# Top-k attention with a low-rank mixer: masking of the probabilities moved from VectorE to GpSimd, row sums to ScalarE

## The chip, the cores and the metric

The kernel runs on one core of one Trainium2 chip. The time is that of one execution on the device, in microseconds (us). The engines have short names: PE is TensorE (matmuls and transposes; PEld is its weight load), DVE is VectorE, ACT is ScalarE, POOL is GpSimd, SP is SyncE, which issues loads.

## The reference

For each of 8 batches and 8 heads (576 rows, 64 columns), attention keeps the 32 largest scores of a row. What follows is an MLP-mixer block on the joined heads.

```python
scores = scale * np.matmul(q, k.transpose(0, 1, 3, 2))
kth = np.partition(scores, -top_k, axis=-1)[..., -top_k:-top_k + 1]
mask = scores >= kth
scores = np.where(mask, scores, -1000000000.0)
scores = scores - np.max(scores, axis=-1, keepdims=True)
attn = np.exp(scores)
attn = attn / (np.sum(attn, axis=-1, keepdims=True) + 1e-09)
out = np.matmul(attn, v)
# x: heads joined, (8, 576, 512)
h = x.transpose(0, 2, 1) @ U @ V          # rank 32
u = x + h.transpose(0, 2, 1)
result = u + np.maximum(u @ w_ch1, 0.0) @ w_ch2
```

## The kernel before

Heads are taken in pairs, so there are 32 pairs, four to a batch. The 576 rows of a pair are five tiles: four of 128 rows and a tail of 64. A *step* is one tile of one pair, 160 in all. A full step has two chunks of 128 x 576 scores, one for each head. A tail step has one chunk, which holds the 64 rows of both heads one above the other. Every five steps are called a *group* here.

A step has a front and a back. The front, `scores` and `select`, makes the scores with four matmuls (L209), copies them to a tile `Ssb` in SBUF on ACT (L219, in the tail L222), and finds the 32nd largest score of each row on DVE: four rounds of the eight largest values (`MAX8`, L233) with three removals of these between them (`MATCH_REPLACE8`, L242, into tiles `rr`). After the first round ACT makes the exponentials `E` (L237, L238). After the last round the eighth value `ms[c][:, 7:8]` is the threshold, and one DVE instruction for each chunk (L245) compares the scores with it, multiplies `E` with the result, and accumulates the row sums, with a small DVE instruction that reads the accumulator out. In the tail step DVE adds 1e-9 to the sum and inverts it (L265, L266), and POOL scales `E` (L267); in full steps this is done later, on the attention's output (L311 to L316).

The back transposes `E` on PE (L288), copies the result on ACT (L289), and multiplies with the values (L295), with a copy of the output on ACT (L304).

The main loop puts the front of step n ahead of the back of step n - 1. Between these, `fill` lays pieces of the MLP of the batch before: w1 matmuls (L382) with a Relu on ACT (L392), and w2 matmuls (L399), whose output DVE adds (L409) and POOL sends out (L411). After the fourth pair of a batch the mixer is laid in (L336, L349, with DVE's additions at L350). In the first 19 steps two pieces of the weights in 64 bits are also rounded in every step, by five DVE and three POOL instructions each (L108 to L124).

PE's instructions stand in the order in which the program names them, so PE meets, in this order: the scores of step n, a piece of MLP, the transposes of step n - 1 with MLP between them, the scores of step n + 1. A PE instruction that waits holds all that is behind it. The other engines have queues that run in order too, but that order is made by a planner, which takes what it reckons to be ready first, by its own costs. Tiles come from pools; `bufs` says how many of one kind are alive at once, and a new tile waits for all readers of the one whose place it takes.

The lines that the change touches are in `scores` and `select`:

Of the kernel before, what the change touches and what calls it, by code (L numbers as in the profile page):

```python
# [8 lines left out]
F32 = mybir.dt.float32  # L9
U32 = mybir.dt.uint32  # L10
AF = mybir.ActivationFunctionType
ALU = mybir.AluOpType
# [8 lines left out]
def kernel(  # L21
# [23 lines left out]
    nc = tc.nc  # L45
    B, H, S, D = q.shape
    P = 128
# [16 lines left out]
    attn = ctx.enter_context(tc.tile_pool(name="attn", bufs=2))  # L64
# [15 lines left out]
    def rows(t):  # L80
        return P if t < NT else TAIL

    def cols(t):
        return slice(t * P, t * P + rows(t))

    def half(h):
        return slice(h * D, (h + 1) * D)
# [112 lines left out]
    def scores(g, t):  # L200


        qkT = qkTs[g]
        n = rows(t)
        S2 = attn.tile([P, 2, S], F32, tag="Ssb", name="Ssb", bufs=2)
        scs = [ps_s.tile([P, 2, 512], F32, tag="sc", name="sc") for _ in range(2)]
        for i, sc in enumerate(scs):
            for h in range(2):
                nc.tensor.matmul(  # L209
                    sc[slice(0, n) if t < NT else half(h), h, 0:HALF],  # L210
                    lhsT=qkT[half(h), 0, cols(t)],
                    rhs=qkT[half(h), 1, i * HALF : (i + 1) * HALF],
                    start=True,
                    stop=True,
                )
        for i, sc in enumerate(scs):
            cs = slice(i * HALF, (i + 1) * HALF)
            if t < NT:
                nc.scalar.copy(S2[:, :, cs], sc[:, :, 0:HALF])  # L219
            else:  # L220
                for h in range(2):
                    nc.scalar.copy(S2[half(h), 0, cs], sc[half(h), h, 0:HALF])  # L222
        return [S2[:, 0], S2[:, 1]] if t < NT else [S2[:, 0]]

    def select(chunks, sums):


        Es = [attn.tile([P, S], F32, tag="E", name="E", bufs=6) for _ in chunks]
        curs, ms = list(chunks), [None] * len(chunks)
        for i in range(TOPK // 8):  # L230
            for c in range(len(chunks)):
                m = small.tile([P, 8], F32, tag="m8", name="m8")
                nc.vector.max(m, curs[c])  # L233
                ms[c] = m
                if i == 0:
                    nmax = small.tile([P, 1], F32, tag="nmax", name="nmax", bufs=4)
                    nc.scalar.mul(nmax, m[:, 0:1], -SCALE)  # L237
                    nc.scalar.activation(Es[c], chunks[c], AF.Exp, bias=nmax, scale=SCALE)  # L238
            if i < TOPK // 8 - 1:
                for c in range(len(chunks)):  # L240
                    nxt = attn.tile([P, S], F32, tag="rr", name="rr", bufs=4)
                    nc.vector.match_replace(nxt, ms[c], curs[c], NEG)  # L242
                    curs[c] = nxt
        for c in range(len(chunks)):
            nc.vector.scalar_tensor_tensor(  # L245
                out=Es[c],
                in0=chunks[c],
                scalar=ms[c][:, 7:8],
                in1=Es[c],
                op0=ALU.is_ge,  # L250
                op1=ALU.mult,
                accum_out=sums[c],
            )
        return Es

    def front(g, t):
        if t == 0:
            dens[g] = small.tile([P, NT, 2], F32, tag="den", name="den", bufs=3)
        chunks = scores(g, t)
        if t < NT:  # L260
            probs[g, t] = select(chunks, [dens[g][:, t, h : h + 1] for h in range(2)])
        else:
            den = small.tile([P, 1], F32, tag="dent", name="dent", bufs=2)
            (E,) = select(chunks, [den])
            nc.vector.tensor_scalar_add(den, den, 1e-9)  # L265
            nc.vector.reciprocal(den, den)  # L266
            nc.gpsimd.tensor_scalar(E, E, den, None, ALU.mult)  # L267
            probs[g, t] = [E]
            del qkTs[g]
# [247 lines left out]
```

## Time and profile before

| | before |
|---|---|
| median of 3 runs | 2250.36 us (2250.21 to 2250.86) |
| profiled execution | 2251.6 us |
| its span | 2249.8 us |
| DVE busy | 1822.1 us (81%) |
| PE busy | 1953.6 us (87%) |
| ACT busy | 866.0 us (38%) |
| POOL busy | 235.5 us (10%) |
| mean granted PE clock | 0.908 |

The profile is one execution. In a row for a group of instructions stand the line, the engine, the operation, what is written and read, and the count; then the busy time in us and the mean duration in ns; then the idle time of the engine just before them and what ended it. In a timeline a row starts with the start and the length in us, and instructions of one kind that follow each other are merged. A row of the windows view has the stretch, its length, the busy time of PE, PEld, DVE, ACT and POOL with the count of instructions, the granted PE clock, the DMA share and GB/s. In the rows with 40 digits each digit is a slice of the span; 9 is a busy share of 90% or more, and for the clock it is tenths of full speed.

### The profile page before, as it was taken

The numbers are of one execution on the slowest core, as the hardware profiler recorded it, in microseconds if no ns is written. First come the engines' busy times: TensorE is split into PE (matmuls) and PEld (weight loads), VectorE is DVE, ScalarE is ACT, GpSimd is POOL, SyncE is SP. The second block draws the span as 40 slices with busy tenths as digits, with TensorE's granted clock in tenths as the row PEclk, the third lists the DMA queues.
The fourth block names the chain that finished last, engine by engine and source line by source line (L and its number), as shares of the span: only waits on it lengthen the run. The fifth ranks groups of instructions, "written<-read, shape, count | busy, mean of one in ns | idle before, by whom it ended". The sixth has DMA issues, their size and how long they took to land.

```text
span 2249.8 us, 27480 instructions
## 1 busy us (share of the span) xinstructions
PE 1953.6 (87%) x10048; PEld 1141.4 (51%) x10048; DVE 1822.1 (81%) x3876; ACT 866.0 (38%) x2001; POOL 235.5 (10%) x186
## 2 busy tenths in 40 slices
PE   5334448999899989999899989999899989999998
PEld 3223234656365645646365645647365645546545
DVE  8999997999599995999599976999699968996000
ACT  3223233445254533444254434444244424443100
POOL 2655530000000000000000000000000000000000
PEclk6556558999899998999899989999899989999999
DMA  3222210100000000010000000000000000000000
GB/s 83 80 76 64 79 35 4 24 27 18 10 21 21 24 21 16 17 28 17 10 22 21 24 16 23 20 26 19 5 22 21 24 16 26 1 10 3 10 12 10
DMA packets 98630, 56.59 MB, mean 25 GB/s; under 512 B 83712, under 2 KB 92064, under 8 KB 98496
## 3 DMA queue, kind: packets, MB, share of 16 engines
q1 hardware_dynamic: 95552, 45.40, 7.6%
q0 software_dynamic: 2944, 9.44, 1.2%
q8 instruction: 79, 1.29, 0.2%
q14 instruction: 55, 0.45, 0.1%
HBM read 45.38 MB, written 9.44 MB: 24 GB/s over the span
## 4 chain that ended last, share of the span: by engine, by line
DVE 46%; PE 36%; issue 13%; ACT 4%; DMA 0%; POOL 0%; SPq 0%; POOLq 0%; DVEq 0%; ACTq 0%
DVE m L233 19%; DVE rr L242 17%; PE mm L399 13%; PE mm L382 8%; PE O L295 5%; DVE E L245 4%; PE sc L209 4%; PE tp L288 3%; PE mm L349 2%; ACT Ssb L219 2%; DVE bits L114 1%; ACT E L238 1%; ACT PT L289 1%; DVE bits L111 1%; DVE X L316 1%
## 5 line engine op out<-in xcount | busy, mean ns | idle before, releaser
L399 PE MATMUL mm<-w,hT 128*128 128x512 f32 (+1 forms) x1280 | 619.0, 616 | 3.5 <-DVE X L350 3.5
L233 DVE MAX8 m<-rr 128x8 f32<-128x576 f32 x864 | 614.1, 747 | 1.9
L382 PE MATMUL mm<-uT,w 128*128 128x256 f32 (+1 forms) x2048 | 545.4, 412 | 1.5 <-ACT hT L392 1.4
L382 PEld LDWEIGHTS mm<-uT,w 128*128 128x128 f32 x2048 | 372.5, 190 | 123.4 <-issue 32.9
L242 DVE MATCH_REPLACE8 rr<-m,rr 128x576 f32<-128x576 f32 x576 | 423.4, 741 | 0.0
L288 PE MATMUL tp<-ident,E 128*128 128x128 f32 (+1 forms) x1440 | 246.9, 299 | 196.2 <-DVE E L245 131.8
L288 PEld LDWEIGHTS tp<-ident,E 128*128 128x128 f32 (+1 forms) x1440 | 175.1, 145 | 343.8 <-DVE E L245 134.8
L399 PEld LDWEIGHTS mm<-w,hT 128*128 128x128 f32 (+1 forms) x1280 | 215.3, 184 | 247.8 <-issue 241.5
L289 ACT COPY PT<-tp 128x512 f32<-128x512 f32 (+1 forms) x448 | 209.5, 495 | 320.0 <-PE tp L288 319.1
L233 DVE MAX8 m<-Ssb 128x8 f32<-128x576 f32 x288 | 205.5, 749 | 137.2 <-ACT Ssb L219 136.0
L295 PE MATMUL O<-PT,va 128*64 128x128 f32 (+3 forms) x3200 | 236.8, 288 | 19.7 <-ACT PT L289 18.9
L295 PEld LDWEIGHTS O<-PT,va 128*64 128x64 f32 (+1 forms) x3200 | 173.0, 146 | 113.4 <-issue 60.1
L245 DVE SCALAR_TENSOR_TENSOR E<-Ssb,m,E 128x576 f32<-128x576 f32 x288 | 223.4, 808 | 3.5
L238 ACT ACTIVATE E<-Ssb,nmax 128x576 f32<-128x576 f32 x288 | 223.0, 774 | 6.4
L392 ACT ACTIVATE hT<-mm 128x320 f32<-128x320 f32 (+1 forms) x256 | 104.3, 407 | 288.7 <-PE mm L382 288.0
L242 DVE MATCH_REPLACE8 rr<-m,Ssb 128x576 f32<-128x576 f32 x288 | 211.8, 742 | 0.0
L209 PE MATMUL sc<-qkT 64*128 64x288 f32 (+1 forms) x1280 | 210.3, 450 | 0.3 <-ACT qkT L188 0.3
L219 ACT COPY Ssb<-sc 128x576 f32<-128x576 f32 x256 | 152.3, 640 | 117.9 <-PE sc L209 115.3
L409 DVE TENSOR_TENSOR ob<-X,mm 128x512 f32<-128x512 f32 (+1 forms) x40 | 27.3, 682 | 188.8 <-PE mm L399 188.8
L209 PEld LDWEIGHTS sc<-qkT 64*128 64x128 f32 (+1 forms) x1280 | 110.0, 187 | 89.7 <-issue 66.2
L237 ACT ACTIVATE nmax<-m 128x1 f32<-128x1 f32 x288 | 56.5, 196 | 232.8 <-DVE m L233 232.3
L267 POOL TENSOR_SCALAR E<-E,dent 128x576 f32<-128x576 f32 x32 | 56.7, 1772 | 802.3 <-DVE dent L266 755.0
(53 smaller groups left out, 976.0 us busy)
## 6 DMA issues: line engine op xcount, KB each, us to landing
raw<-in_moe_w_ch_dram SPq DMA_DIRECT2D x32, 512.0 KB, 3.7
ld_q<-in_q_dram SPq DMA_DIRECT2D x64, 128.0 KB, 2.7
ld_k<-in_k_dram SPq DMA_DIRECT2D x64, 128.0 KB, 2.7
va<-in_v_dram SPq DMA_DIRECT2D x64, 128.0 KB, 2.1
out_dram<-ob POOLq DMA_DIRECT2D x32, 256.0 KB, 2.6
ld_q<-in_q_dram SPq DMA_DIRECT2D x32, 32.0 KB, 2.4
ld_k<-in_k_dram SPq DMA_DIRECT2D x32, 32.0 KB, 2.4
va<-in_v_dram SPq DMA_DIRECT2D x32, 32.0 KB, 2.2
```

The costliest lines, as they stand in the source:

```text
L209: nc.tensor.matmul(sc[slice(0, n) if t < NT else half(h), h, 0:HALF], lhsT=qkT[half(h), 0, cols(t)], rhs=qkT[half(h), 1, i * HALF : (i + 1 ...
L219: nc.scalar.copy(S2[:, :, cs], sc[:, :, 0:HALF])
L233: nc.vector.max(m, curs[c])
L238: nc.scalar.activation(Es[c], chunks[c], AF.Exp, bias=nmax, scale=SCALE)
L242: nc.vector.match_replace(nxt, ms[c], curs[c], NEG)
L245: nc.vector.scalar_tensor_tensor(out=Es[c], in0=chunks[c], scalar=ms[c][:, 7:8], in1=Es[c], op0=ALU.is_ge, op1=ALU.mult, accum_out=sums[c],)
L288: nc.tensor.transpose(tp[0 : rows(j), j - j0, h, :], E[:, cols(j)], ident)
L289: nc.scalar.copy(PT[0:n, j0 : js[-1] + 1, 0:nh, :], tp[0:n, 0 : len(js)])
L295: nc.tensor.matmul(O[half(h), 0:m], lhsT=va[0 : rows(j), h, j, :], rhs=PT[0 : rows(j), j, h, :] if nh == 2 else PT[0 : rows(j), j, 0, half ...
L382: nc.tensor.matmul(ph[:, 0:width], lhsT=w1[:, cc, f * P : (f + 1) * P], rhs=uT[:, cc, 0:width], start=(cc == 0), stop=(cc == NC - 1),)
L392: nc.scalar.activation(hTs[f][:, 0:width], ph[:, 0:width], AF.Relu)
L399: nc.tensor.matmul(po[0:n, :], lhsT=hTs[f][:, offs[t] : offs[t] + n], rhs=w2[:, f, :], start=(f == 0), stop=(f == NF - 1),)
```

## The change

For each chunk the one DVE instruction is replaced by three on other engines: POOL compares the scores with the threshold into a new tile `top`, POOL multiplies `E` by it, and ACT copies `E` onto itself while it accumulates the row sum. `Ssb` gets a third buffer, and `rr` has three instead of four.

```diff
-        S2 = attn.tile([P, 2, S], F32, tag="Ssb", name="Ssb", bufs=2)
+        S2 = attn.tile([P, 2, S], F32, tag="Ssb", name="Ssb", bufs=3)
...
-                    nxt = attn.tile([P, S], F32, tag="rr", name="rr", bufs=4)
+                    nxt = attn.tile([P, S], F32, tag="rr", name="rr", bufs=3)
...
         for c in range(len(chunks)):
-            nc.vector.scalar_tensor_tensor(
-                out=Es[c],
-                in0=chunks[c],
-                scalar=ms[c][:, 7:8],
-                in1=Es[c],
-                op0=ALU.is_ge,
-                op1=ALU.mult,
-                accum_out=sums[c],
-            )
+            top = attn.tile([P, S], F32, tag="top", name="top")
+            nc.gpsimd.tensor_scalar(top, chunks[c], ms[c][:, 7:8], None, ALU.is_ge)
+            nc.gpsimd.tensor_tensor(Es[c], Es[c], top, ALU.mult)
+            nc.scalar.activation(Es[c], Es[c], AF.Copy, accum_out=sums[c])
         return Es
```

## The prediction

> **What bounds the kernel now.** I read the page's engine rows and its slices first.
>
> ```profile
> PE 1953.6 (87%) x10048; PEld 1141.4 (51%) x10048; DVE 1822.1 (81%) x3876; ACT 866.0 (38%) x2001; POOL 235.5 (10%) x186
> PE   5334448999899989999899989999899989999998
> DVE  8999997999599995999599976999699968996000
> PEclk6556558999899998999899989999899989999999
> ```
>
> There are three stretches. Up to 327 us (steps 0 to 19) DVE is full, PE half idle. From there to 2060 us both are nearly full. The last 190 us are MLP on PE alone. In the middle a batch of 20 steps holds three ordinary five-step groups of 54.6, 56.0, 54.6 us (mean 55.1, from the timeline) and one of 83.6 us in which the mixer runs: seven batches, so 21 ordinary groups and 7 of the other kind. The windows view takes one ordinary group, then two clock windows:
>
> ```profile
> 650.40:705.00 54.60, 52.83 (x299) 31.31 (x298) 52.27 (x114) 26.61 (x62) 1.75 (x2) 1.00 0.08 22
> 1088.10:1091.52 3.42, 1.98 (x4) 0.66 (x4) 3.42 (x8) 0.17 (x1) 0.00 (x0) 1.00 0.00 0
> 1091.52:1094.93 3.41, 1.14 (x2) 0.63 (x3) 2.81 (x7) 0.00 (x0) 0.00 (x0) 0.50 0.00 0
> ```
>
> PE is busy 52.83 and DVE 52.27 of 54.60 us: neither has room. The other two rows show what a gap costs: PE was busy 1.98 of 3.42 us, and the next window's granted clock was 0.50.
>
> Next, the order of one step, on PE (scores, transposes, scores two steps on) and on DVE (first maximum, the two maskings, the next step's first maximum), and who waited in 345 to 2054 us:
>
> ```profile
> 650.44 1.24 PE L209 MATMUL sc<-qkT 64*128 64x288 f32 x8
> 663.82 1.15 PE L288 MATMUL tp<-ident,E 128*128 128x128 f32 x8
> 671.41 1.24 PE L209 MATMUL sc<-qkT 64*128 64x288 f32 x8
> ```
> ```profile
> 652.45 1.42 DVE L233 MAX8 m<-Ssb 128x8 f32<-128x576 f32 x2 [2.83 <-ACT Ssb L219]
> 662.11 0.80 DVE L245 SCALAR_TENSOR_TENSOR E<-Ssb,m,E 128x576 f32<-128x576 f32 x1
> 662.84 0.81 DVE L245 SCALAR_TENSOR_TENSOR E<-Ssb,m,E 128x576 f32<-128x576 f32 x1
> 664.18 1.41 DVE L233 MAX8 m<-Ssb 128x8 f32<-128x576 f32 x2
> ```
> ```profile
> PE tp L288 <- DVE E L245: 7.4, 24, 0.7
> ```
>
> Masking ends at 663.65 and the transposes start at 663.82; still PE waited only 7.4 us for E in 1700. E arrives just in time, with no reserve. The ring is: scores to first maximum 2.0; to the end of the last maximum (662.19) 9.7; to the transposes 1.6; to the scores two steps on 7.6. That is 20.9 us for two steps, while DVE needs 22.8 for them (652.45 to 675.29). So DVE sets the pace by 1.9 us, and PE's own work (21.0, 650.44 to 671.41) is as close behind.
>
> **Prices.** From the groups, shapes kept apart:
>
> ```profile
> L245 DVE SCALAR_TENSOR_TENSOR E<-Ssb,m,E 128x576 f32<-128x576 f32 x288 | 223.4, 808 | 3.5
> L238 ACT ACTIVATE E<-Ssb,nmax 128x576 f32<-128x576 f32 x288 | 223.0, 774 | 6.4
> L219 ACT COPY Ssb<-sc 128x576 f32<-128x576 f32 x256 | 152.3, 640 | 117.9 <-PE sc L209 115.3
> L267 POOL TENSOR_SCALAR E<-E,dent 128x576 f32<-128x576 f32 x32 | 56.7, 1772 | 802.3 <-DVE dent L266 755.0 <-PE O L295 23.7 <-PE mm L399 17.4
> L121 POOL TENSOR_SCALAR mask<-mask 128x512 f32<-128x512 f32 x32 | 64.5, 2016 | 109.5 <-DVE mask L119 109.5
> L124 POOL TENSOR_TENSOR w<-bits,mask 128x512 f32<-128x512 f32 x32 | 42.8, 1336 | 2.5
> ```
>
> *Removed:* 288 maskings and accumulator reads, 223.4 + 23.4 = 247 us of DVE, 1.5 us of a full step.
>
> *Compare:* same operation, shape and column operand as L267, whose median is 1.72. Ends: 1.43 (were it as quick as a product) and 2.27 (2016 scaled by 576/512; L121 runs against DVE). I take 1.72. *Product:* L124's undisturbed 1.27 scaled by 576/512 is 1.43. *Row sum on ACT:* between the 0.64 of L219 and the 0.77 of L238; 0.70 and 0.10 for the accumulator (0.08 on DVE). ACT gains 230 us on 866 and stays far from full.
>
> *The chain of a full step,* from the end of the second chunk's last maximum: the first chunk's is 0.66 earlier, start on POOL 0.20 (dent at 1010.37, L267 at 1010.57), compare 1.72, hand-over 0.07, product 1.43, the same 3.22 for the second chunk, to ACT 0.15, row sum 0.80, to PE 0.10. Sum 7.0, where now it is 1.6: PE's transposes read what ACT writes, so they wait for all of it. Tail step (one chunk): 0.20 + 3.22 + 0.95, then add, reciprocal, L267 and hand-overs 2.5: 6.9 against 3.4 now.
>
> *Buffers:* with three rr, the fourth and sixth MATCH_REPLACE8 output reuses a tile read by the instruction just before; 0 to 0.14 each (tail step's spacing 0.80 against 0.66), I take 0.1, so the 9.7 becomes 9.9. The third Ssb lets the next copies go while POOL still reads; without it that read would hold them.
>
> *The ring after:* 2.0 + 9.9 + 7.0 + 7.6 = 26.5 us for two steps, above DVE's (about 20) and PE's 21.0. So PE idles 5.5 us per two steps. The row at 1088.10 says that 1.44 idle in a window halves the clock. At the batch change PE restarted at 605.65 and had 1.00 back at 610.2: 4.6 us at half speed lose 2.3. This lies in the stretch from transposes to scores: 28.8. Tail ring, from step 74: copies done 2.4 after the scores (1000.49 to 1002.85), maxima 5.5 (1002.88 to 1009.05 less an output add of 0.67), 6.9, and 5.7 to the scores (1014.8 to 1020.5): 20.5, with clock 22.8. Ten steps are eight full and two tail legs on two chains: (8 x 28.8 + 2 x 22.8)/2 = 138.0, or 69.0 per group, 13.9 more than 55.1. Times 21: +292.
>
> The Trainium skill ("TensorE: Matmul & The Clock Gate", Part 1) has the half clock come after an idle window of about 3.4 us; the row above fell with 1.98 us busy, so the row decides. By the page alone shorter gaps would keep the clock, which is the first rival's sum.
>
> The Trainium skill ("GPSIMD Engine Reference", Engine selection) calls one-input work on GPSIMD roughly line-rate; L267's 1.72 against MAX8's 0.75 on as many elements denies it. With a compare of about 0.7, the estimate by that page, a full leg is 2.0 shorter and the total some 95 us lower.
>
> *Mixer groups:* their first two steps have E ready 22 to 30 us ahead (580.0 against 605.7), so nothing is added; the last three are ordinary: 0 to 3 x 2.8; I take 4, times 7: +28.
>
> *First stretch:* DVE does the step, then rounds two weights. Here it shares something with POOL:
>
> ```profile
> 152.90 0.68 DVE L111 SCALAR_TENSOR_TENSOR bits<-raw,bits 128x512 uint32<-128x512 uint32 x1
> 153.50 1.48 DVE L119 TENSOR_SCALAR mask<-raw 128x512 uint32<-128x512 uint32 x1
> ```
> ```profile
> 151.37 2.06 POOL L121 TENSOR_SCALAR mask<-mask 128x512 f32<-128x512 f32 x1 [8.88 <-DVE mask L119]
> 153.41 1.29 POOL L118 TENSOR_TENSOR bits<-bits,last 128x512 uint32<-128x512 uint32 x1
> ```
>
> L119 takes 1.48 beside POOL's two-input operation, 0.41 alone; L111 beside the one-input one keeps its 0.68. MAX8 and MATCH_REPLACE8 don't change beside either. Masks now run just when DVE rounds: two products cost 1.1 each, against 1.3 saved (1.5 less 0.2): +0.9 on 16 steps, about +15. Ends: -21 (nothing blocked) and +81 (all 6.4 us blocked).
>
> *Queues.* On ACT the row sum stands before PT, hT and Ssb copies, for which PE and DVE wait; at nothing if it is placed where its product is ready. On DVE the tail's add now waits for ACT with the next maxima behind it: 0 to 4.4; taken at 0, as DVE would have 4 us idle per step. On POOL the output DMAs stand behind up to 6.4 us of masks; ob has two buffers, and nothing else needs them.
>
> Sum: the profiled execution took 2251.6 (span 2249.8); + 292 + 28 + 15 = 2586.6. The median of the runs, 2250.36, is 1.2 below that execution: 2585.
>
> **Rivals.** (1) *The clock stays at 1.00* because the idle comes in small pieces: groups (8 x 26.5 + 2 x 20.5)/4 = 63.3, 21 x 8.2 = +172; mixer groups half, +14; first +15: 2451. For: 5.5 us over two steps may split. Against: 1.44 us suffices. (2) *ACT stuck behind the row sum:* the MLP group between scores and transposes (2.3 us at 651.61) can no longer run while E is awaited: +2.3 per leg, ten legs on two chains make two groups, so 10 x 2.3/4 = 5.75 per group, 121 in all: 2706. For: ACT is in order. Against: now its copies come in order of readiness. (3) *Faster: E's delay is hidden,* DVE's relief counts: ordinary groups fall to PE's busy 53.7, -1.5 x 21 = -31; first -21: 2198. It decides if E comes within 2 us after the last maximum; a compare alone takes 1.72 and four passes are queued, and PE's order has no other work to put there.
>
> **How the numbers follow.** Forecast 0.66; (1) 0.16; (2) 0.12; (3) 0.04; results in between 0.02, half of them no change. A change below 0.2% couldn't be told from none. A chain longer by d moves full legs by d, tail legs by d/2: (8d + d)/4 x 21 = 47d. Both compares at 1.43 give -27, at 2.27 give +52. With the first stretch (-36 and +66 from the value taken) the forecast's own span is about 2520 to 2700, since the ends rarely meet. To leave out no more than 2 in 10 the range takes in rivals 1 and 2: 2440 to 2710.
>
> **To look for.** Right: PE waits for E of ACT, hundreds of us, PE busy share falls; clock digits of 7 to 9 where they were 9; ordinary groups near 69 us; POOL near 1140 us (235 + 288 x 3.15); the last maximum to the transposes 7 us. Wrong: groups under 60 us, or POOL passes under 1 us.

## The result and the profile after

The changed kernel takes 2680.93 us (median of 4 runs, 2674.54 to 2682.92), against 2250.61 us for the kernel before in the same session. The ratio is 1.191, with a 95% interval of 1.189 to 1.193. The forecast of 2585 us had the direction; of the 430 us that were lost it had 335. The profiled execution after took 2681.29 us (span 2679.5), at a mean granted clock of 0.853. One of the four executions of `no_sum_lag2` below took 3311 us, at a granted clock of 0.55, and is left out of that kernel's time.

The first view is the page after: engine rows and slices, to be laid beside those of before.

```profile
PE 2100.3 (78%) x10048; PEld 1215.3 (45%) x10048; DVE 1652.3 (62%) x3300; ACT 1073.1 (40%) x2577; POOL 1132.3 (42%) x762
...
PE   4334478788888888788887887888887888787999
...
DVE  8999956666466646666566656656566664666100
...
POOL 5888834443344334443344433344243433444000
PEclk7555569889889889998898979989898888899899
```

PE's digits fell from 9 to 8 and 7, DVE's from 9 to 6, and POOL never gets above 4 in the middle. No engine is full any more, so the kernel waits on a chain. PE has the same 10048 instructions, but they are busy 147 us longer (2100.3 against 1953.6), at a mean granted clock of 0.853 instead of 0.908. The waits name the chain. A row has who waited for whom, then the sum in us, the number of waits and the longest.

```profile
POOL top L246 <- DVE m L233: 728.5, 116, 23.3
ACT E L248 <- POOL E L247: 578.5, 217, 9.6
PEld tp L283 <- ACT E L248: 511.4, 178, 13.2
PE tp L283 <- ACT E L248: 436.1, 162, 12.5
DVE m L233 <- ACT Ssb L219: 427.7, 82, 16.2
```

PE waited 7.4 us for E in the middle of the kernel before; the fourth row has 436.1, 301.4 of them between 360 and 2480 us. The first row costs nothing: POOL has time to spare. The second row is a wait that the forecast's sum put at nothing: ACT, whose queue also holds the copies that PE and DVE need, stands still for 578.5 us until POOL's product is done. The groups by form give the prices:

```profile
L246 POOL TENSOR_SCALAR top<-Ssb,m 128x576 f32<-128x576 f32 x288 | 503.1, 1747 | 1048.0 <-DVE m L233 728.5 <-PE sc L209 112.3 <-PE mm L394 48.6
L247 POOL TENSOR_TENSOR E<-E,top 128x576 f32<-128x576 f32 x288 | 410.2, 1424 | 22.6
L248 ACT ACTIVATE E<-E 128x576 f32<-128x576 f32 x288 | 196.7, 683 | 579.2 <-POOL E L247 578.5
L248 ACT ACTIVATION_READ_ACCUMULATOR E<-E 128x1 f32 x288 | 54.0, 188 | 0.0
```

One step of the timeline shows both effects: first POOL, then PE, then ACT.

```profile
820.98 1.73 POOL L246 TENSOR_SCALAR top<-Ssb,m 128x576 f32<-128x576 f32 x1 [8.79 <-DVE m L233]
822.79 1.41 POOL L247 TENSOR_TENSOR E<-E,top 128x576 f32<-128x576 f32 x1
824.17 1.73 POOL L246 TENSOR_SCALAR top<-Ssb,m 128x576 f32<-128x576 f32 x1
825.99 1.40 POOL L247 TENSOR_TENSOR E<-E,top 128x576 f32<-128x576 f32 x1
```
```profile
806.41 1.24 PE L209 MATMUL sc<-qkT 64*128 64x288 f32 x8
...
825.07 0.47 PE L283 MATMUL tp<-ident,E 128*128 128x128 f32 x1 [3.96 <-ACT E L248]
828.25 0.90 PE L283 MATMUL tp<-ident,E 128*128 128x128 f32 x3 [2.71 <-ACT E L248]
```
```profile
809.13 0.68 ACT L248 ACTIVATE E<-E 128x576 f32<-128x576 f32 x1 [4.25 <-POOL E L247]
809.72 0.19 ACT L248 ACTIVATION_READ_ACCUMULATOR E<-E 128x1 f32 x1
809.82 1.16 ACT L219 COPY Ssb<-sc 128x576 f32<-128x576 f32 x2
...
827.42 0.68 ACT L248 ACTIVATE E<-E 128x576 f32<-128x576 f32 x1 [2.31 <-POOL E L247]
828.01 0.19 ACT L248 ACTIVATION_READ_ACCUMULATOR E<-E 128x1 f32 x1
```

*The chain.* The last maximum of the step ends at 821.48 on DVE. Four passes on POOL end at 827.39, ACT sums from 827.42 to 828.20, and PE takes the second chunk's transposes at 828.25: 6.8 us behind the maximum, 2.71 of them as a second wait of PE after one of 3.96.

*The queue.* The scores that PE made from 806.41 to 807.65 are copied by ACT only at 809.82. ACT had stood 4.25 us before a row sum whose product was not ready, with the copies behind it. DVE's next maximum needs the copies. The Trainium skill ("Perfetto Trace Analysis", Tensor Engine Instruction) says that ACT, DVE and GpSimd take their instructions strictly in order; these rows agree, with 2.2 us between the end of the scores and their copy.

Where the 430 us lie, by the starts of the scores (one stretch is a row; the sum of the differences is that of the spans, 429.7):

| stretch | before | after | difference |
|---|---|---|---|
| up to step 20 | 327.3 | 342.7 | +15.4 |
| 20 ordinary groups | 55.5 each | 72.6 each | +341.6 |
| 7 groups with the mixer | 81.1 each | 88.6 each | +52.5 |
| from step 155 (the last ordinary group, then MLP) | 244.3 | 264.4 | +20.1 |

One ordinary group in the windows view (length, busy PE, PEld, DVE, ACT, POOL, granted clock, DMA share, GB/s) says the same as the whole; the kernel before had 52.83 and 52.27 us of PE and DVE in 54.60, at a clock of 1.00:

```profile
736.40:806.40 70.00, 58.07 (x297) 34.26 (x296) 46.71 (x96) 32.64 (x81) 27.76 (x19) 0.90 0.07 17
```

### The profile page after: what moved, and what is told of

Its sections match the earlier page's. It is cut to its first block, busy times and chain, and to the rows that moved or that the text cites. A ratio compares the mean times of both kernels' runs of the same rounds, so it can differ in the third digit from the quotient of the medians.

```text
span 2679.5 us, 28343 instructions
## 1 busy us (share of the span) xinstructions
PE 2100.3 (78%) x10048; PEld 1215.3 (45%) x10048; DVE 1652.3 (62%) x3300; ACT 1073.1 (40%) x2577; POOL 1132.3 (42%) x762
## 4 chain that ended last, share of the span: by engine, by line
PE 31%; DVE 29%; POOL 21%; issue 10%; ACT 8%; POOLq 0%; DMA 0%; SPq 0%; ACTq 0%; DVEq 0%
DVE m L233 12%; DVE rr L242 12%; POOL top L246 11%; POOL E L247 9%; PE mm L377 9%; PE mm L394 7%; PE tp L283 4%; PE O L290 4%; ACT E L248 4%; PE sc L209 2%; ACT Ssb L219 2%; PE mm L344 2%; PE tp L187 1%; DVE bits L114 1%; DVE mask L119 1%
## 5 line engine op out<-in xcount | busy, mean ns | idle before, releaser
L246 POOL TENSOR_SCALAR top<-Ssb,m 128x576 f32<-128x576 f32 x288 | 503.1, 1747 | 1048.0 <-DVE m L233 728.5
L283 PE MATMUL tp<-ident,E 128*128 128x128 f32 (+1 forms) x1440 | 295.3, 337 | 495.4 <-ACT E L248 436.1
L394 PE MATMUL mm<-w,hT 128*128 128x512 f32 (+1 forms) x1280 | 663.8, 654 | 0.0
L377 PE MATMUL mm<-uT,w 128*128 128x256 f32 (+1 forms) x2048 | 585.4, 435 | 0.0
L283 PEld LDWEIGHTS tp<-ident,E 128*128 128x128 f32 (+1 forms) x1440 | 201.2, 163 | 683.8 <-ACT E L248 511.4
L377 PEld LDWEIGHTS mm<-uT,w 128*128 128x128 f32 x2048 | 400.5, 204 | 133.8 <-issue 45.3
L248 ACT ACTIVATE E<-E 128x576 f32<-128x576 f32 x288 | 196.7, 683 | 579.2 <-POOL E L247 578.5
L247 POOL TENSOR_TENSOR E<-E,top 128x576 f32<-128x576 f32 x288 | 410.2, 1424 | 22.6
L394 PEld LDWEIGHTS mm<-w,hT 128*128 128x128 f32 (+1 forms) x1280 | 229.0, 195 | 262.9 <-issue 259.1
L284 ACT COPY PT<-tp 128x512 f32<-128x512 f32 (+1 forms) x448 | 210.5, 496 | 201.7 <-PE tp L283 200.3
L290 PE MATMUL O<-PT,va 128*64 128x128 f32 (+3 forms) x3200 | 239.4, 290 | 19.1 <-ACT PT L284 18.8
L290 PEld LDWEIGHTS O<-PT,va 128*64 128x64 f32 (+1 forms) x3200 | 174.6, 147 | 113.4 <-issue 68.2
L406 POOL DMA_DIRECT2D out_dram<-ob x32 | 19.4, 606 | 370.4 <-DVE ob L404 370.4
```

The costliest lines, as they stand in the source:

```text
L246: nc.gpsimd.tensor_scalar(top, chunks[c], ms[c][:, 7:8], None, ALU.is_ge)
L247: nc.gpsimd.tensor_tensor(Es[c], Es[c], top, ALU.mult)
L248: nc.scalar.activation(Es[c], Es[c], AF.Copy, accum_out=sums[c])
L283: nc.tensor.transpose(tp[0 : rows(j), j - j0, h, :], E[:, cols(j)], ident)
L284: nc.scalar.copy(PT[0:n, j0 : js[-1] + 1, 0:nh, :], tp[0:n, 0 : len(js)])
L290: nc.tensor.matmul(O[half(h), 0:m], lhsT=va[0 : rows(j), h, j, :], rhs=PT[0 : rows(j), j, h, :] if nh == 2 else PT[0 : rows(j), j, 0, half ...
```

## The experiments

The ratio is each time against the kernel before on the same chip, which took 2250.7 to 2251.8 us there.

### The buffers alone

The edit is shown against the kernel before; masks and sums stay on DVE.

```diff
-tag="Ssb", name="Ssb", bufs=2)
+tag="Ssb", name="Ssb", bufs=3)
...
-tag="rr", name="rr", bufs=4)
+tag="rr", name="rr", bufs=3)
```

> The kernel before with only the buffer counts of the change (Ssb 3, rr 3). Theory A (the loss comes from E arriving late in a ring that had no reserve): E is as early as before, so 2250 to 2268 us; the upper end is 0.2 us per full step of DVE for the two MATCH_REPLACE8 that reuse a tile just read. Rival B (half clock) and rival C (POOL's passes slow the others while they run) expect the same, 2250 to 2268, as no wait and no POOL work is added. Over 2290 would blame the buffers.

Measured: 2233.73 us, ratio 0.992 (0.990 to 0.993). Ordinary groups take 56.1 us, mixer groups 76.1 instead of 81.1. So the two buffer changes together gain 17 us: 5 us in each of the seven mixer groups, against half a microsecond lost in each ordinary group and 4 us in the first stretch. What POOL and ACT do to the kernel has to be counted from 2234: it is 447 us.

### The row sums left out, and the row sums beside the chain

```diff
-            nc.scalar.activation(Es[c], Es[c], AF.Copy, accum_out=sums[c])
+            nc.vector.memset(sums[c], 1.0)                                    # no_sum
+            nc.scalar.activation(top, Es[c], AF.Copy, accum_out=sums[c])      # sum_aside
```

> The changed kernel with the row sums left out (the denominators are set to 1, so the output is not scaled); compare and product stay on POOL. Theory A: E is 1.0 us earlier and ACT's queue is free, so the scores' copies come back from 3.5 to about 2.2 us after the scores: leg 30.0 - 1.0 - 1.3 = 27.7 us for two steps, ordinary groups 72.6 to about 66, total near 2545 (2500 to 2590). Rival B (the clock alone): the waits stay above 1.4 us, so the clock falls as often and the time stays within 40 us of 2681. Rival C (POOL work as such): POOL does the same, so 2660 to 2690.

Measured: 2517.37 us, ratio 1.119 (1.117 to 1.120).

> The changed kernel, but ACT's row-sum pass writes to the mask's tile instead of E, so PE's transposes wait for POOL's product and no longer for ACT; ACT's queue is as full as in the change. Theory A: only the chain is 0.95 us shorter in full steps: 0.95 x 2 x 21 = 40 us less, 2640 (2620 to 2660). If ACT's queue order is nearly all of ACT's part, less than 15 us change. Rival B and C: 2670 to 2690.

Measured: 2640.34 us, ratio 1.173 (1.171 to 1.174).

The sums cost 164 us in all (2681 - 2517). Only 41 of them are the length of the sum itself in the chain, since 2640 is what is left when PE no longer waits for ACT's write. The other 123 come back only when the sums leave ACT's queue. In `no_sum` DVE begins its first maximum 2.1 us after PE begins the scores, where DVE has been idle; it is 3.6 in the changed kernel and 2.0 before.

ACT's queue is not the only one that `no_sum` frees. In the changed kernel DVE adds 1e-9 to a group's denominators (L306) when ACT has summed, and waits for it:

```profile
DVE den L306 <- ACT E L248: 52.8, 23, 11.2
```

In the trace 30.6 us of these waits, in steps 20 to 154, lie between the first and the last maximum of a step, so they lengthen the chain. The 123 us hold both queues, and no run parts them.

And 284 us remain above the buffers alone without any row sum. PE's waits in `no_sum` show whose they are; 213.7 of the 350.4 us lie between 345 and 2320 us:

```profile
PE tp L283 <- POOL E L247: 350.4, 130, 11.5
```

### Twelve idle matmuls ahead of the transposes

```diff
+        if nh == 2 and g >= 4 and not (g % NPAIR == 0 and t < 2):
+            warm = ps_t.tile([P, NT, P], F32, tag="tp", name="warm")
+            for i in range(12):
+                nc.tensor.matmul(warm[:, i % NT, :], lhsT=ident, rhs=ident, start=True, stop=True)
```

> The changed kernel with 12 matmuls of the identity by itself, into a PSUM tile that nothing reads, ahead of the transposes of 100 full steps (not in the first four pairs, nor in the two steps of a batch whose E is ready early). They take 2.6 us at full clock and fill part of PE's wait, so that the clock should stay at 1.00 more often. Theory A (ring, with some 2 us of half clock in each leg): ordinary groups from 72.6 to 68 or 69, total 2600 (2570 to 2640), half-clock time well under 461 us. Rival B (the clock is most of the loss): below 2500. If PE's time, not its waits, were the bound, 100 x 2.6 = 260 us more: 2940. If the clock doesn't matter: 2670 to 2700.

Measured: 2939.99 us, ratio 1.306 (1.304 to 1.308). This failed as a test of the clock. The matmuls stand ahead of 98 full steps' transposes. PE was at half clock for 428 us between steps 20 and 155, not much less than the changed kernel's 461 there, and still waited 249.1 us for E behind the added matmuls. ACT's queue was later still: it stood 911.1 us for POOL's product instead of 578.5, and the 256 Relus started 534 us in sum behind the end of their matmuls, against 220 in the changed kernel. The share of the clock stays unmeasured by a run of its own.

### The product made twice

```diff
             nc.gpsimd.tensor_tensor(Es[c], Es[c], top, ALU.mult)
+            nc.gpsimd.tensor_tensor(Es[c], Es[c], top, ALU.mult)
```

> The change with POOL's product done twice (the mask is 0 or 1, so the values don't change): 1.42 us more per chunk, 2.8 per full step. Theory A with the slope of the prediction (8 legs of 2.8 and 2 of 1.4 on two chains and two groups, 6.3 us per ordinary group, 132 in all), mixer groups +12, first stretch +35 where two more products hold DVE: 2860 (2800 to 2900). Rival C (throughput of POOL): POOL is busy 42% and would be 57%, no change in the middle: 2700 to 2730.

Measured: 2876.71 us, ratio 1.278 (1.276 to 1.280), 196 us above the changed kernel. The last maximum is 10.1 us ahead of the transposes that wait, instead of 7.0, and ordinary groups take 78.8 us. The chain's length is what PE pays.

### The row sums moved to ACT, the mask left on DVE

```diff
                 op1=ALU.mult,
-                accum_out=sums[c],
             )
+            nc.scalar.activation(Es[c], Es[c], AF.Copy, accum_out=sums[c])
```

> The change's buffers and its row sums on ACT, but compare and product stay in the one DVE instruction (without its accumulator). E is then 1.0 us later than before instead of 5.4. Theory A: ring 2.0 + 9.9 + 2.7 + 7.6 = 22.2 us for two steps, still under DVE's 22.8 and close to it: 2230 to 2300. Rival D (ACT's queue is stuck whenever it holds a row sum): the 164 us that leaving the sums out has saved come with the sums alone: near 2400. Rival B: no waits, 2230 to 2260.

(The buffers are those of the change.) Measured: 2255.70 us, ratio 1.002 (1.001 to 1.003), 22 us above the buffers alone. The same 288 sums cost 22 us behind a quick mask and 164 behind POOL's. What costs is not the work on ACT but what it waits for.

### Transposes one step later, with the mask on POOL and on DVE

```diff
-    for n in range(STEPS + 1):
+    for n in range(STEPS + 2):
...
-        gb, tb = divmod(n - 1, CH)
+        gb, tb = divmod(n - 2, CH)
...
-        if n >= 1:
+        if n >= 2:
```

(E gets eight buffers for that; with the mask on POOL, `top` then has one and `nmax` two.)

> The change, with the transposes of a tile one step later (the back of step n - 2 instead of n - 1, so E has a whole step more), eight E tiles, one mask tile, two nmax. POOL and ACT do the same work as in the change. Theory A (E late in a ring without reserve, and ACT's queue with it): the ring now spans three steps, 3.5 + 10.4 + 7.5 + 8.6 = 30 us, or 10 per step, under what DVE (10.4) and PE (10.7) need, so PE doesn't wait for E and ordinary groups are 53.5 to 56 us; total 2220 to 2290. Rival B (the clock): follows A, as without waits the clock stays at 1.00. Rival D (ACT stuck behind the row sum, whatever the reserve): Relus and PT copies are still late, total over 2400. Rival C (POOL's passes as such slow DVE and ACT): over 2500.

Measured: 2622.10 us, ratio 1.165 (1.163 to 1.167).

> The kernel before with Ssb 3, rr 3, eight E tiles and the transposes one step later; masking as before on DVE. Theory A: DVE sets the pace of the ordinary groups (56 us) and PE hardly waits for E, so a step more of reserve gives little: 2215 to 2240, against 2234 without it. If lag2 is faster than this one, DVE's relief of 1.5 us per full step is worth something once the delay is covered; theory A expects up to 1.3 us x 84 full steps = 110 us at most, PE's own 53.5 us per group limiting it to 50.

Measured: 2239.24 us, ratio 0.995 (0.993 to 0.996); ordinary groups take 55.9 us. So the later transposes do hardly any harm by themselves (2239 against 2234), but with the mask on POOL they gain only 59 us. A late E alone can't be the whole cause. The waits of `lag2` say what took its place (L284 copies the transposed probabilities, L290 multiplies with the values):

```profile
ACT E L248 <- POOL E L247: 622.0, 244, 8.7
...
PEld O L290 <- ACT PT L284: 184.6, 109, 6.1
...
PE tp L283 <- ACT PT L284: 146.3, 78, 5.7
...
PE O L290 <- ACT PT L284: 136.6, 65, 5.8
```

PE has its E now, and waits for ACT's copies instead. The timeline of `lag2` has them behind an exponential and a row sum, which stands behind POOL; a start is followed by the length:

```profile
805.24 0.68 ACT L248 ACTIVATE E<-E 128x576 f32<-128x576 f32 x1 [1.63 <-POOL E L247]
...
806.82 0.72 ACT L284 COPY PT<-tp 128x512 f32<-128x512 f32 x2
```
```profile
807.44 1.50 PE L290 MATMUL O<-PT,va 128*64 128x64 f32 x20 [4.17 <-ACT PT L284]
```

### Both causes taken away

The later transposes, and no row sums (the `memset` of `no_sum`).

> The kernel of lag2 with the row sums left out (denominators set to 1, so the output is not scaled): E has a whole step more and no row sum stands in ACT's queue. Theory E (two causes: E late in a ring without reserve, some 280 us, and ACT's queue held by row sums that wait for POOL, some 160 us with one step and nearly all with two): both are gone, so 2190 to 2260. Rival C (POOL's passes as such slow the others): they run as in the change, so over 2400. Theory A alone has already failed at lag2 (2622).

Measured: 2203.87 us (2203.3 to 2204.4), ratio 0.979 (0.978 to 0.981). Ordinary groups take 55.1 us. PE no longer waits for E between 330 and 2000 us, and the largest that is left there is for the mixer's addition on DVE:

```profile
PE mm L344 <- DVE X L345: 33.5, 19, 5.4
```

POOL is as busy as in the changed kernel (1137.6 us). So POOL's work as such doesn't slow the kernel. Four kernels make a square: with the sums 2681 and, one step later, 2622; without them 2517 and 2204. Each remedy alone gains 59 or 164 us, both together 477. The two causes cover for each other, and either one alone keeps the kernel above 2500.

### Row sums issued late

```diff
-            nc.scalar.activation(Es[c], Es[c], AF.Copy, accum_out=sums[c])
...
+        if n >= 2:
+            if g < NP:
+                with tc.issue_after(last_copy[0].ins):
+                    row_sums(gb, tb)
```

(`row_sums` holds the sums and, in a tail step, the add, the reciprocal and POOL's scaling; `last_copy` is ACT's last copy of the newest scores. That is `lag2_late`; `lag1_late` has the same with the transposes and the buffers of the change.)

> The whole computation: lag2, with the row sums (in the tail step the add, reciprocal and scaling too) put behind the score copies of two steps later in ACT's queue, when POOL has long finished. Theory E: ACT no longer waits there, so 2195 to 2270; DVE's relief could bring it under bufs_only's 2234, as PE's work alone is 53.5 us of an ordinary group. Rival D' (ACT's passes cost by their time, not by their waits): as ACT does the same passes, near 2600. Rival C: over 2400.

Measured: 2506.03 us, ratio 1.113 (1.112 to 1.115).

> The change with the row sums put behind the score copies of the next step in ACT's queue; transposes one step later as in the change, buffers as in the change. Theory E: E's delay stays and the sum is in its path, the Ssb copies and most Relus are no longer behind it: between no_sum plus its chain (2517 + 40 = 2557) and the change: 2540 to 2620. If the place in ACT's queue doesn't matter: 2670 to 2690.

Measured: 2766.09 us, ratio 1.229 (1.227 to 1.231).

Both missed. ACT was freed in `lag2_late` (its wait for POOL's product is 65.7 us), but the tail step's scaling had moved behind the sums, and PE's transposes of the tail wait for it, 224.2 of 327.4 us between 340 and 2300; L260 is the scaling, L291 the transposes:

```profile
PE tp L291 <- POOL E L260: 327.4, 31, 35.5
```

In `lag1_late` the same wait is 274.1 us, and another 307.8 for full steps' E. The edit had put one more thing late than it was meant to.

### The version that leaves the tail step as it was

```diff
+        if len(chunks) == 1:
+            nc.vector.scalar_tensor_tensor(out=Es[0], in0=chunks[0], scalar=ms[0][:, 7:8],
+                in1=Es[0], op0=ALU.is_ge, op1=ALU.mult, accum_out=sums[0])
+            return Es
```

(Add, reciprocal and scaling stand behind it again; full steps keep POOL's mask, the later transposes and the late row sums.)

> The version with the transposes one step later and the row sums issued behind the copies of the scores of two steps on (2506 us) waited for the scaling of the short step's probabilities, 31 times by 10 to 11 us, because the row sum that this scaling divides by was issued late as well. Here the short steps are masked and summed on VectorE by the one pass of the kernel before, and their add, reciprocal and scaling stand right behind it; the full steps keep the mask and the product on GpSimd and the late row sums on ScalarE. Theory of two causes (a ring without a reserve, and a ScalarE queue that the row sums hold while they wait for GpSimd): with both out of the way the time lies between the kernel with a later transpose and no row sums (2204) and the changed buffers alone with VectorE's mask (2234), give or take 20: 2185 to 2255. The groups of an ordinary pair then take 54 to 57 us, and no wait of TensorE for a copy or for E is above 100 us in sum. Rival, that the row sums cost what they cost wherever they stand (ScalarE's 0.87 us each, 256 of them, on the path): 2204 + 220 = 2420 or more. Rival, that a late issue of the row sums is itself what cost 300 us in the version before (the copies of the transposed probabilities queue behind them): about 2500 again, with TensorE waiting for those copies.

Measured: 2233.87 us, ratio 0.992 (0.991 to 0.994), ordinary groups 55.4 us. Both rivals fall: 256 row sums on ACT and 512 passes on POOL are there, and the time is that of the buffers alone, and 447 us below the changed kernel. Its ordinary group in the windows view shows why it isn't better still:

```profile
645.90:701.00 55.10, 54.30 (x309) 33.59 (x307) 46.94 (x97) 32.37 (x80) 28.28 (x18) 1.00 0.07 17
```

DVE has 8 us of room, which is what the change was able to free, and PE has 0.8. In this group PE is the bound, and the room is worth nothing. Nothing that does the whole work beat the buffers alone (2233.73) by more than can be told apart.

## Why the prediction was right, and where a term was mis-sized

*The mechanism* was the forecast's: E arrived just in time before, and its delay opens a ring of two steps that no engine's load explains. `no_sum_lag2` shows it from the other side. A step of reserve takes the cost away, once ACT is free too. But the forecast's sum held one cause of two. `no_sum` with the 41 us of the sum's own length put back is an estimate of the delay without the queues: some 2560 us, near the 2585 of the forecast; what the sum lacked is the queues.

*The legs.* A leg goes from the scores of a step to the scores two steps on. These are means, in us, over the 74 full steps (14 tail steps) whose leg lies outside of the mixer's groups:

| part of a full leg | forecast | measured |
|---|---|---|
| scores to first maximum | 2.0 | 3.46 |
| to the end of the last maximum | 9.9 | 10.36 |
| to the second chunk's transposes | 7.0 | 7.62 |
| to the scores two steps on, with the clock | 9.9 | 8.75 |
| sum | 28.8 | 30.2 |
| tail leg | 22.8 | 24.35 |

By the prediction's own formula the measured legs make (8 x 30.2 + 2 x 24.35)/4 = 72.6 us, which is the measured group; the forecast was 69.0, from 55.1 before, where the mean of the 20 groups is 55.5. The 21 ordinary groups cost +362 (341.6 and, for the one behind step 155, its stretch's 20.1) instead of +292; that is the largest part of what was missed. The forecast's 9.9 us for the last part were too much, and hid some of what the other parts lacked.

*The term that was mis-sized* is the one under queues: ACT's row sum "at nothing if it is placed where its product is ready". It wasn't placed there. ACT stood for 578.5 us, and the queues' share of the time is 123 us by `no_sum` and `sum_aside`. The parts of the legs in `no_sum` show where the row sums' 164 us lie. A full leg is 1.6 us shorter there: 0.6 ahead of the first maximum (2.84 instead of 3.46), 0.65 in the chain to the transposes, 0.3 behind them. A tail leg is 3.0 us shorter: 1.4 in the maxima (5.81 instead of 7.25, where DVE's L306 had waited) and 1.6 in the chain. So only 0.6 of the 1.46 us that the first line of the table has above the forecast are copies behind a sum. The rest is there without the sums too: the 2.0 had been read where DVE stood idle, and the mean over the same steps of the kernel before is 3.28. The other term for a queue, DVE's add in the tail step (L260), was rightly taken at nothing in the middle: it waited 114.3 us between 360 and 2480, but the next maximum still began right behind ACT's copies.

The second rival had ACT stuck behind the row sum: with the forecast's other terms it gave 2706, by a term of 121 us. That 121 is so near 123 is luck, since that rival had put its price on MLP matmuls which can't run between scores and transposes. The Relus were late by 220 us in sum (66 before), but the scores' copies and DVE's add count too. ACT's wait should not have been a rival with 0.12, but a part of the forecast. The reason given against it, that ACT's copies come in order of readiness, was read from a kernel in which nothing on ACT waited for POOL.

*The clock* was priced too high: 2.3 us in each leg, while the last part of the leg grew from 7.66 to 8.75, so by 1.1. The trace says why. The prediction took one window with 1.98 of 3.42 us busy as the rule. In steps 20 to 155 after, of the windows at full clock with under 42% busy, 62 of 63 were followed by half clock; with 42 to 60% it was 2 of 17; above that 1 of 392. Two windows, each with the next:

```profile
865.62:869.03 3.41, 1.61 (x8) 1.08 (x6) 3.31 (x7) 1.01 (x4) 3.33 (x3) 1.00 0.39 89
869.03:872.44 3.41, 0.33 (x1) 0.14 (x1) 0.82 (x2) 1.74 (x5) 3.39 (x3) 1.00 0.17 38
841.72:845.13 3.41, 1.26 (x9) 0.93 (x9) 3.38 (x7) 1.93 (x6) 1.40 (x1) 1.00 0.00 0
845.13:848.54 3.41, 3.41 (x5) 0.60 (x5) 3.38 (x8) 1.37 (x3) 0.21 (x1) 0.50 0.01 2
```

After 1.61 busy us the next window had 1.00, after 1.26 it had 0.50. In this trace a gap mostly had to take some 2 us out of one window, not 1.44. The turn isn't sharp, nor the same in both kernels: in steps 20 to 155 before, windows at full clock with under 42% busy were followed by half clock in 8 of 8 cases, those with 42 to 60% in 6 of 11, and none above that; the prediction's row is one of the 6. The Trainium skill ("TensorE: Matmul & The Clock Gate", Part 1) has the half clock follow an idle window; that is stricter than the trace, where a window with 1.26 us of work was followed by it. The first rival, a clock that stays at 1.00, is wrong all the same: 461 us at half clock against 143, between steps 20 and 155. How many of the 430 us this is was not isolated; PE's busy time grew by 147 us, and not all of that is on the chain.

*Right to a tenth:* the compare (1.747 us, 1.72 taken), the product (1.424 against 1.43), the chain where PE waits (6.95 against 7.0), POOL's total (1132.3 against 1140). ACT's pass and its accumulator read overlap and take 0.78 us from start to end (809.13 to 809.91), where 0.80 was taken.

*Right by luck:* the first stretch has +15.4, where +15 was forecast from POOL's products holding DVE. In `no_sum`, with the same passes on POOL, it is 330.4, only 3.1 above the kernel before. In the changed kernel DVE also waits 16.2 us for ACT's sums in this stretch (L260 and L306), which the forecast took at nothing, and its rounding of weights takes 20 us longer instead of 35.

*Mis-sized besides:* mixer groups +52.5, where +28 was forecast (46 of it goes with the row sums: 82.1 us each in `no_sum`); and the buffers, which the prediction let cost 0.2 us a step and which gain 17 us together. Which of the two kinds does what, no run separated.

*The third rival* (2198, E's delay hidden) gave nearly the number of a kernel that does hide it, 2204; but that one leaves the row sums out, and `lag2_tail_dve`, which does all the work, takes 2234. Its condition, E within 2 us of the last maximum, wasn't met: in `no_sum` the second chunk's transposes still come 6.0 us behind it, where PE waits. A later transpose gave the reserve that the condition asked of the chain.

## What to carry to other kernels

Work moved off a full engine is worth its time only if what it makes has a reserve: look at the wait of its consumer (7.4 us in 1700 here, with hardly any gap between the masking's end and the transposes), and count the moved work's whole latency against that. Then ask of each queue that the moved work enters what it waits for and who is queued behind: 288 row sums of 0.8 us, on an engine that is 40% busy, cost 164 us behind POOL, and 22 behind DVE. When two such causes exist, taking one away shows little; only the run without both shows what each hid.

## What the runs showed of the hardware that was not expected

- ACT's read of the accumulator takes 188 ns, DVE's took 81 (23.4 us for 288); the pass itself, SBUF to SBUF over 128 x 576 f32, takes 683, and the two overlap by some 90.
- The clock's fall follows how busy a window of 3.41 us is, with the turn at about 42% in this kernel's trace; in the kernel before, 6 of 11 windows between 42 and 60% were followed by half clock too.
